# A gated delta rule with an SMELU MLP on one core: list scheduling of all orders, 32-bit transposes and block inverses by substitution

## The chip, the cores and the metric

The kernel runs on one core of one Trainium2 chip. The metric is device time in microseconds (us) from launch to end; a run's own span, from its first to its last instruction, is about 1.7 us shorter. PE is TensorE (PEld its weight loads), DVE is VectorE, ACT is ScalarE, POOL is GpSimd, SP is SyncE, which only issues DMAs. ACT, PE and SP with a "q" behind the name are the sequencers issuing something. Lnnn is a line of the kernel that the profile belongs to. A "step" is 32 tokens of the recurrence; there are 24, and four batches of eight heads run side by side. An execution is called slow when it took over 1.5% longer than the fastest of the same kernel, and fast otherwise; ratios use fast executions alone.

## The reference

```python
def _attn_ref(q, k, v, beta, g):          # B, H, S, D = 4, 8, 768, 48
    k_n = k / (np.linalg.norm(k, axis=-1, keepdims=True) + 1e-06)
    state = np.zeros((B, H, D, D)); y = np.zeros_like(q)
    for t in range(S):
        readout = einsum('bhd,bhde->bhe', q[:, :, t], state)
        y[:, :, t] = g[:, :, t] * readout
        v_old = einsum('bhde,bhd->bhe', state, k_n[:, :, t])
        state = state + beta[:, :, t] * outer(k_n[:, :, t], v[:, :, t] - v_old)
    return y

def _moe_ref(x, w_in, w_out):             # 3072 tokens, 384 -> 2048 -> 384
    h = x @ w_in
    g = where(h >= 1, h, where(h <= -1, 0, (h + 1) ** 2 / 4))
    return g @ w_out
# out = _moe_ref(_attn_ref(...) as [B*S, H*D])
```

The recurrence is computed 32 tokens at a time. Each step needs the Gram matrix of its keys, the inverse of a 32x32 unit-triangular matrix for each of the 32 batch-head pairs, and four products with a 48x48 state. All of these are 32x32 matmuls: 32 to 64 of them for one logical product. The MLP is ordinary large matmuls on the readouts.

## The kernel before

A pair of steps is inverted by four Newton levels, each of two products with a copy through ACT or DVE behind each. The MLP has two PSUM buffers and starts when four steps are done. The framework's scheduler decides the order.

```python
    psS = ... bufs=1   # state
    psN = ctx.enter_context(tc.tile_pool(name="psN", bufs=2, space=bass.MemoryType.PSUM))   # Gram, Newton
    psC = ctx.enter_context(tc.tile_pool(name="psC", bufs=2, space=bass.MemoryType.PSUM))   # chain
    psM = ctx.enter_context(tc.tile_pool(name="psM", bufs=2, space=bass.MemoryType.PSUM))   # MLP
    # [...]
    def newton_pair(p):
        # [...]
        for lv in range(4):
            ep = psN.tile([128, 2, J, 32], FP, name=f"ep{p}_{lv}", tag="n")
            # [4 matmuls put 2*I into ep]
            for c in range(2):
                for j in range(J):
                    for h4 in range(4):
                        r = slice(32 * h4, 32 * h4 + 32)
                        nc.tensor.matmul(ep[r, c, j], zc[c][r, j], al[c][r, j], start=False, stop=True, ...)
            e16 = nwt.tile([128, 2, J, 32], F16, ...)
            nc.scalar.copy(out=e16[:], in_=ep[:])
            zp = psN.tile([128, 2, J, 32], FP, name=f"zp{p}_{lv}", tag="n")
            # [64 matmuls more, zp = e16^T zc, then a copy to z16 on DVE or ACT]
    # [...]
    def mlp_in(gi, xt, m):
        hp = psM.tile([128, NT], FP, name=f"hp{gi}_{m}", tag="m")      # NT = 512 tokens
        for kt_ in range(3):
            nc.tensor.matmul(hp[:], win[:, kt_, m * 128:m * 128 + 128], xt[:, kt_]..., ...)
        rl = ...; nc.scalar.activation(out=rl[:], in_=hp[:], func=AF.Relu, bias=c_half[:], scale=0.5)
        if m % 2 == 0:      # DVE: max, then min and product
            # [...]
        else:               # POOL squares, DVE finishes
            # [...]
    # [mlp_out: 16 matmuls of 384 columns for each of 4 token tiles]
    # [...]
    for s in range(NSTEP):
        xt = chain_step(s)
        if s % 2 == 1:
            parallel(s // 2 + 2)          # loads, Gram, Newton of a later pair
        # [a share of the MLP tasks of the last complete group of four steps]
```

Of the kernel before, what the change touches and what calls it, by code (L numbers as in the profile page):

```python
# [9 lines left out]
U16 = mybir.dt.uint16  # L10
# [3 lines left out]


def _ap(t, dims, off=0):

    a = t[:]
    return bass.AP(tensor=a.tensor, offset=a.offset + off, ap=[list(a.ap[0])] + [list(d) for d in dims])


@with_exitstack
def kernel(
# [20 lines left out]
    NM = DFF // 128  # L44
    assert D == 48 and H == 8 and B == 4

    const = ctx.enter_context(tc.tile_pool(name="const", bufs=1))
    raw = ctx.enter_context(tc.tile_pool(name="raw", bufs=2))
    prep = ctx.enter_context(tc.tile_pool(name="prep", bufs=2))
    small = ctx.enter_context(tc.tile_pool(name="small", bufs=2))  # L50
    ktp = ctx.enter_context(tc.tile_pool(name="ktp", bufs=4))
    nwt = ctx.enter_context(tc.tile_pool(name="nwt", bufs=3))
    zfp = ctx.enter_context(tc.tile_pool(name="zfp", bufs=3))
    chn = ctx.enter_context(tc.tile_pool(name="chn", bufs=2))
    xtp = ctx.enter_context(tc.tile_pool(name="xtp", bufs=2))
    mlpt = ctx.enter_context(tc.tile_pool(name="mlpt", bufs=4))
    mlpg = ctx.enter_context(tc.tile_pool(name="mlpg", bufs=28))
    outp = ctx.enter_context(tc.tile_pool(name="outp", bufs=3))
    psS = ctx.enter_context(tc.tile_pool(name="psS", bufs=1, space=bass.MemoryType.PSUM))
    psN = ctx.enter_context(tc.tile_pool(name="psN", bufs=2, space=bass.MemoryType.PSUM))  # L60
    psC = ctx.enter_context(tc.tile_pool(name="psC", bufs=2, space=bass.MemoryType.PSUM))
    psM = ctx.enter_context(tc.tile_pool(name="psM", bufs=2, space=bass.MemoryType.PSUM))


    HS = 4 * S * D
    raws = {}

    def load(s0, n):

        ts = {}  # L70
        for nm, src in (("k", k), ("q", q), ("v", v), ("g", g)):
            t = raw.tile([128, GS, J, D], FP, name=f"r{nm}{s0}", tag=f"raw_{nm}")
            ts[nm] = t
        raws[s0] = ts

    def load_part(s0, off, n, names):
        ts = raws[s0]
        for nm, src in (("k", k), ("q", q), ("v", v), ("g", g)):
            if nm not in names:
                continue  # L80
            for h4 in range(4):
                for c in range(off, off + n):
                    a = bass.AP(tensor=src.tensor, offset=src.offset + h4 * S * D + (s0 + c) * C * D,
                                ap=[[D, C], [HS, J], [1, D]])
                    nc.sync.dma_start(out=ts[nm][32 * h4:32 * h4 + 32, c, :, :], in_=a)  # L85


    braw = const.tile([128, NG, C], FP, name="braw")
    for h4 in range(4):
        for j in range(J):  # L90
            a = bass.AP(tensor=beta.tensor, offset=beta.offset + h4 * S + j * 4 * S,
                        ap=[[C, GS], [GS * C, NG], [1, C]])
            nc.sync.dma_start(out=braw[32 * h4 + 4 * j:32 * h4 + 4 * j + 4, :, :], in_=a)  # L93
    load(0, GS)
    load_part(0, 0, 2, "k")
    load_part(0, 0, 2, "qv")

    ones = const.tile([128, 32], FP, name="ones")
    nc.gpsimd.memset(ones[:], 1.0)
    id32 = const.tile([128, 32], FP, name="id32")  # L100
    upf = const.tile([128, 32], F16, name="upf")
    lof = const.tile([128, 32], F16, name="lof")
    for h4 in range(4):
        r = slice(32 * h4, 32 * h4 + 32)
        nc.gpsimd.affine_select(out=id32[r, :], in_=ones[r, :], compare_op=ALU.is_equal, fill=0.0,
                                base=0, pattern=[[-1, 32]], channel_multiplier=1)
        nc.gpsimd.affine_select(out=upf[r, :], in_=ones[r, :], compare_op=ALU.is_gt, fill=0.0,
                                base=0, pattern=[[1, 32]], channel_multiplier=-1)
        nc.gpsimd.affine_select(out=lof[r, :], in_=ones[r, :], compare_op=ALU.is_gt, fill=0.0,
                                base=0, pattern=[[-1, 32]], channel_multiplier=1)  # L110
    i16 = const.tile([128, 32], F16, name="i16")
    nc.gpsimd.tensor_copy(out=i16[:], in_=id32[:])
    two_i = const.tile([128, 16, 32], F16, name="two_i")
    nc.gpsimd.tensor_scalar(out=two_i[:], in0=_ap(id32, [[0, 16], [1, 32]]), scalar1=2.0, scalar2=None, op0=ALU.mult)
    upmask = const.tile([128, J, 2, 32], F16, name="upmask")
    nc.gpsimd.tensor_copy(out=upmask[:].rearrange("p j a c -> p (j a) c"), in_=_ap(upf, [[0, 2 * J], [1, 32]]))
    lomask = const.tile([128, J, 32], F16, name="lomask")
    nc.gpsimd.tensor_copy(out=lomask[:], in_=_ap(lof, [[0, J], [1, 32]]))
    c_half = const.tile([128, 1], FP, name="c_half")
    nc.gpsimd.memset(c_half[:], 0.5)  # L120


    NZM, NA = 6, 4
    zms, als = [], []
    for i in range(NZM):
        t = const.tile([128, J, 2, 32], F16, name=f"zm{i}")
        nc.gpsimd.memset(t[:], 0.0)
        nc.gpsimd.tensor_scalar(out=t[:, :, 0, :], in0=_ap(id32, [[0, J], [1, 32]]), scalar1=-1.0, scalar2=None, op0=ALU.mult)
        zms.append(t)
    for i in range(NA):  # L130
        t = const.tile([128, J, 32], F16, name=f"al{i}")
        nc.gpsimd.tensor_copy(out=t[:], in_=_ap(id32, [[0, J], [1, 32]]))
        als.append(t)
    kqs = []
    for i in range(4):
        t = const.tile([128, 2, J, 4, 32], F16, name=f"kq{i}")
        nc.gpsimd.memset(t[:], 0.0)
        kqs.append(t)

    sb = const.tile([128, NG, J, GS], FP, name="sb")  # L140
    bt = const.tile([128, NG, C], FP, name="bt")
    nc.vector.transpose(out=bt[:].rearrange("p a b -> p (a b)"), in_=braw[:].rearrange("p a b -> p (a b)"))  # L142
    nc.scalar.activation(out=sb[:].rearrange("p a b c -> p (a b c)"), in_=bt[:].rearrange("p a b -> p (a b)"), func=AF.Sqrt)

    load_part(0, 2, 2, "kqv")
    load_part(0, 0, 4, "g")


    win = const.tile([128, 3, DFF], F16, name="win")
    wout = const.tile([128, NM, DM], F16, name="wout")  # L150

    def load_weights():
        for h4 in range(4):
            for p0, kt, h2, e0, n in ((0, 0, 0, 0, 32), (0, 1, 0, 32, 16), (16, 1, 1, 0, 16), (0, 2, 1, 16, 32)):
                r0 = (h2 * 4 + h4) * D + e0
                nc.gpsimd.dma_start(out=win[32 * h4 + p0:32 * h4 + p0 + n, kt, :], in_=moe_w_in[r0:r0 + n, :])  # L156
        nc.gpsimd.dma_start(out=wout[:], in_=moe_w_out.rearrange("(m p) n -> p m n", p=128))


    st = {}  # L160

    def prep_pair(p):
        s0 = 2 * p
        gi, off = s0 // GS, s0 % GS
        rw = raws[gi * GS]
        kr = rw["k"][:, off:off + 2]
        sbv = _ap(sb, [[1, 2], [GS, J]], gi * J * GS + off)
        ksq = prep.tile([128, 2, J, D], FP, name=f"ksq{p}", tag="ksq")
        nc.gpsimd.tensor_tensor(out=ksq[:], in0=kr, in1=kr, op=ALU.mult)  # L169
        nsq = small.tile([128, 2, J], FP, name=f"nsq{p}", tag="nsq")  # L170
        nc.vector.tensor_reduce(out=nsq[:], in_=ksq[:], axis=AX.X, op=ALU.add)  # L171
        nrm = small.tile([128, 2, J], FP, name=f"nrm{p}", tag="nrm")
        nc.scalar.activation(out=nrm[:], in_=nsq[:], func=AF.Sqrt)
        nre = small.tile([128, 2, J], FP, name=f"nre{p}", tag="nre")
        nc.vector.tensor_scalar(out=nre[:], in0=nrm[:], scalar1=1e-6, scalar2=None, op0=ALU.add)
        rcp = small.tile([128, 2, J], FP, name=f"rcp{p}", tag="rcp")
        nc.vector.reciprocal(out=rcp[:], in_=nre[:])
        rs = small.tile([128, 2, J], FP, name=f"rs{p}", tag="rs")
        nc.vector.tensor_tensor(out=rs[:], in0=rcp[:], in1=sbv, op=ALU.mult)  # L179
        kq = kqs[p % 4]  # L180
        kqf = kq[:].rearrange("p s j a t -> p (s j) (a t)")
# [4 lines left out]
        for c in range(2):  # L186
            nc.gpsimd.tensor_tensor(out=vt[:, c], in0=rw["v"][:, off + c],
                                    in1=_ap(sb, [[GS, J], [0, D]], gi * J * GS + off + c), op=ALU.mult)
        st[p] = dict(kq=kq, vt=vt, kt=[], zm=[], al=[])

    def gram_step(p, c):
        d = st[p]
# [208 lines left out]
```

## Time and profile before

Median 608.07 us (five runs, 603.64 to 611.33), profiled span 600.9 us, mean granted clock 0.730.

| | before |
|---|---|
| PE matmuls, busy | 14,496, 364.9 us (61%) |
| DVE, ACT, POOL busy | 37%, 25%, 25% |
| first matmul, last matmul, end of span | 34.3, 597.6, 600.9 us |
| sum over blocks of 256 PE instructions of max(3.6 us, own run time) | 499 us (own run time alone: about 350) |
| rest between first and last matmul | 64 us |

The sum in the fourth row is called the block sum below. A block's own run time in it is an estimate: 0.0080 or 0.0125 us for each small matmul with its weight load, at full or half clock, and 0.216 us for 512 columns of a large one at full clock (rates from these traces). The "rest" is the time from the first matmul's start to the last one's end, less the block sum, and the "tail" is what follows the last matmul. A recount with the same rates came within about 2% of every block sum given here; the 350 hangs more on how the matmuls that put 2*I into ep, four side by side, are counted (a recount gives 319 to 389).

From the page: the matmul row, the queue table and the shares of the chain of waits. In the queue table the columns are packets, MB, and share of 16 DMA engines' span.

```profile
PE 364.9 (61%) x14496; PEld 213.9 (36%) x14496; DVE 222.2 (37%) x360; ACT 149.5 (25%) x253; POOL 147.7 (25%) x168
...
q8 instruction: 113, 1.85, 1.3%
...
issue 42%; PE 24%; SPq 9%; POOL 8%; DVE 7%; ACT 5%; DMA 4%; POOLq 0%; ACTq 0%
```

No engine is full, and the chain leads with "issue": time in which an engine waited for nothing that the profile shows. The 14,496 matmuls and as many weight loads are 28,992 PE instructions; 28,992 / 256 = 113.25, and there are 113 packets of 1.85 MB / 113 = 16 KB.

The timeline of PE inside a stretch of small matmuls (start, us, what; in brackets, idle time before it and what ended it):

```profile
175.15 0.32 PE L226 MATMUL ep_2_3853<-al_213,z_1_3851 32*32 32x32 f16 x21 [1.15 <-issue]
175.31 0.43 PE L226 MATMUL ep_2_3853<-al_215,z_1_3851 32*32 32x32 f16 x32
175.56 0.49 PE L292 MATMUL yp_4297<-s_3320,kt_2196 32*32 32x48 f16 x30
176.51 0.53 PE L234 MATMUL zp_2_3924<-z_1_3851,e_2_3922 32*32 32x32 f16 x45 [0.46 <-ACT e_2_3922 L228]
178.88 0.32 PE L234 MATMUL zp_2_3924<-z_1_3851,e_2_3922 32*32 32x32 f16 x19 [1.84 <-issue]
...
182.33 0.23 PE L297 MATMUL yp_4297<-u_4229,zm_203 32*32 32x48 f16 x5 [1.47 <-issue]
...
186.06 0.23 PE L263 MATMUL kp_4449<-s_4295,kt_2265 16*32 16x48 f16 x5 [2.36 <-issue]
```

Count from one "issue" to the next: 21 + 32 + 30 + 45 = 128 matmuls, that is 256 instructions with their weight loads. Even a single product (L234) is cut in the middle, 45 matmuls before the stop and 19 after. The restarts lie 3.73, 3.45 and 3.73 us apart, though the work between them needs about 1.6 us (estimate: 128 times 0.0125). The reading from this is that a block of 256 PE instructions costs about 3.6 us or its own run time, whichever is longer.

The other loss, in the MLP's last group (same columns):

```profile
572.00 0.81 PE L316 MATMUL hp_7_16626<-xt_15576,win 128*128 128x512 f16 x3 [1.97 <-DVE gt_5_16612 L328]
572.65 0.81 PE L316 MATMUL hp_8_16636<-xt_15576,win 128*128 128x512 f16 x3
575.49 0.81 PE L316 MATMUL hp_9_16646<-xt_15576,win 128*128 128x512 f16 x3 [2.03 <-DVE gt_7_16632 L328]
```

Two tiles run, then PE waits 2 us for the DVE operation that frees a PSUM buffer two tiles back: 3.49 us for two tiles that need 1.3.

### The profile page before, as it was taken

Reading aid. Unit: us, or ns where it says so; the run is one execution under the profiler, and the core shown is the slowest. Engines: PE = TensorE matmul, PEld = TensorE weight load, DVE = VectorE, ACT = ScalarE, POOL = GpSimd, SP = SyncE. Lnnn points to the kernel's source line nnn. Section 1 sums busy time; section 2 is a strip of 40 time slices with the busy share of each in tenths; the row PEclk is TensorE's granted clock in tenths of the full one; section 3 lists DMA queues with packets and bytes.
Section 4 is the critical chain, followed back from the end, with each engine's and each line's share of the span. In section 5 each row is a group of like instructions: output and inputs, shape, how many; then the busy total and the mean of one; then the engine's idle time right before and its main releaser. Section 6 shows DMA issues by size and latency. Waiting matters only on the chain.

```text
span 600.9 us, 30600 instructions
## 1 busy us (share of the span) xinstructions
PE 364.9 (61%) x14496; PEld 213.9 (36%) x14496; DVE 222.2 (37%) x360; ACT 149.5 (25%) x253; POOL 147.7 (25%) x168
## 2 busy tenths in 40 slices
PE   0033544658745647646877566877476875678637
PEld 0022433214433413433443443444333533444314
DVE  0131312655102435313744224744037542254351
ACT  1001111421221222222313133313234122243331
POOL 9962000635000122100611102502014321022220
PEclk9999999967855555556585557885558965578899
DMA  1797433550100000024430024410034400000101
GB/s 21 133 177 123 72 73 70 99 98 17 34 5 4 3 0 5 3 47 77 76 76 3 5 60 87 78 55 4 4 75 84 108 4 4 17 5 15 39 1 52
DMA packets 111629, 28.81 MB, mean 48 GB/s; under 512 B 106000, under 2 KB 111120, under 8 KB 111504
## 3 DMA queue, kind: packets, MB, share of 16 engines
q1 hardware_dynamic: 108800, 23.72, 20.1%
q0 software_dynamic: 2704, 3.15, 3.3%
q8 instruction: 113, 1.85, 1.3%
q14 instruction: 12, 0.10, 0.1%
HBM read 25.26 MB, written 4.72 MB: 50 GB/s over the span
## 4 chain that ended last, share of the span: by engine, by line
issue 42%; PE 24%; SPq 9%; POOL 8%; DVE 7%; ACT 5%; DMA 4%; POOLq 0%; ACTq 0%
SPq L85 8%; DMA rg_139<-in_g_dram 2%; SPq L93 2%; PE sps L280 1%; DMA rk_136<-in_k_dram 1%; DMA rv_138<-in_v_dram 1%; PE op_3_6904 L334 1%; PE op_0_9639 L334 1%; PE op_0_12434 L334 1%; PE op_1_6864 L334 1%; PE op_2_6884 L334 1%; PE op_3_16776 L334 0%; PE op_2_16756 L334 0%; PE op_3_16536 L334 0%; PE op_2_16516 L334 0%
## 5 line engine op out<-in xcount | busy, mean ns | idle before, releaser
L316 PEld LDWEIGHTS <-win 128*128 128x128 f16 x288 | 31.6, 117 | 105.7 <-issue 95.8
L203 PE MATMUL gp_291<-kt_289 32*32 32x64 f16 (+1 forms) x64 | 1.0, 236 | 34.3 <-DVE kt_289 L195 34.3
L182 POOL TENSOR_TENSOR kq_217<-rk_4716,rs_4794 128x768 f16<-128x768 f32 x1 | 1.5, 1475 | 56.6 <-DVE rs_4794 L179 56.6
L203 PEld LDWEIGHTS <-kt_289 32*32 32x32 f16 (+1 forms) x64 | 0.9, 122 | 34.3 <-DVE kt_289 L195 34.3
L327 POOL TENSOR_TENSOR r_1_4415<-rl_1_4412 128x512 f32<-128x512 f32 x1 | 1.1, 1050 | 47.1 <-ACT rl_1_4412 L319 47.1
L221 PEld LDWEIGHTS <-i_181 32*32 32x32 f16 x192 | 5.8, 96 | 10.1 <-DVE al_209 L209 5.2
L327 POOL TENSOR_TENSOR r_11_8621<-rl_11_8618 128x512 f32<-128x512 f32 x1 | 1.0, 1038 | 33.6 <-ACT rl_11_8618 L319 33.6
L280 PEld LDWEIGHTS <-kq_221 32*32 32x32 f16 x384 | 5.8, 107 | 7.4 <-issue 7.4
L156 POOL DMA_DIRECT2D win<-in_moe_w_in_dram x16 | 8.2, 516 | 0.0
L327 POOL TENSOR_TENSOR r_5_15903<-rl_5_15900 128x512 f32<-128x512 f32 x1 | 1.0, 1039 | 27.3 <-ACT rl_5_15900 L319 27.3
L280 PEld LDWEIGHTS <-kq_217 32*32 32x32 f16 x384 | 5.9, 110 | 5.0 <-issue 5.0
L327 POOL TENSOR_TENSOR r_5_13883<-rl_5_13880 128x512 f32<-128x512 f32 x1 | 1.0, 1038 | 26.1 <-ACT rl_5_13880 L319 26.1
L327 POOL TENSOR_TENSOR r_7_11108<-rl_7_11105 128x512 f32<-128x512 f32 x1 | 1.0, 1038 | 25.8 <-ACT rl_7_11105 L319 25.8
L171 DVE TENSOR_REDUCE nsq_274<-ksq_272 128x16 f32<-128x768 f32 x1 | 1.0, 954 | 13.6 <-POOL ksq_272 L169 13.6
L182 POOL TENSOR_TENSOR kq_219<-rk_136,rs_1006 128x768 f16<-128x768 f32 x1 | 1.5, 1474 | 16.4 <-DVE rs_1006 L179 16.4
L280 PEld LDWEIGHTS <-kq_219 32*32 32x32 f16 x384 | 4.5, 104 | 2.9 <-issue 2.9
L142 DVE STREAM_TRANSPOSE bt<-braw 128x192 f32<-128x192 f32 x1 | 0.4, 379 | 13.2 <-DMA braw<-in_beta_dram 13.2
L238 DVE CAST z_2_839<-zp_2_774 128x512 f16<-128x512 f32 x1 | 0.7, 692 | 12.3 <-PE zp_2_774 L234 12.3
L327 POOL TENSOR_TENSOR r_1_15595<-rl_1_15592 128x512 f32<-128x512 f32 x1 | 1.0, 1039 | 16.8 <-ACT rl_1_15592 L319 16.8
L327 POOL TENSOR_TENSOR r_1_12800<-rl_1_12797 128x512 f32<-128x512 f32 x1 | 1.0, 1039 | 16.1 <-ACT rl_1_12797 L319 16.1
L280 PEld LDWEIGHTS <-kq_223 32*32 32x32 f16 x320 | 3.7, 101 | 2.9 <-issue 2.9
L238 DVE CAST z_2_1563<-zp_2_1498 128x512 f16<-128x512 f32 x1 | 0.7, 690 | 10.6 <-PE zp_2_1498 L234 10.6
(1828 smaller groups left out, 1186.1 us busy)
## 6 DMA issues: line engine op xcount, KB each, us to landing
wout<-in_moe_w_out_dram POOLq DMA_DIRECT2D x1, 1536.0 KB, 16.4
win<-in_moe_w_in_dram POOLq DMA_DIRECT2D x8, 128.0 KB, 4.5
rk_136<-in_k_dram SPq DMA_DIRECT2D x16, 48.0 KB
rq_137<-in_q_dram SPq DMA_DIRECT2D x16, 48.0 KB
rv_138<-in_v_dram SPq DMA_DIRECT2D x16, 48.0 KB
rg_139<-in_g_dram SPq DMA_DIRECT2D x16, 48.0 KB
rk_2111<-in_k_dram SPq DMA_DIRECT2D x16, 48.0 KB
rq_2112<-in_q_dram SPq DMA_DIRECT2D x16, 48.0 KB
```

The lines of the kernel that those rows point to most:

```text
L85: nc.sync.dma_start(out=ts[nm][32 * h4:32 * h4 + 32, c, :, :], in_=a)
L93: nc.sync.dma_start(out=braw[32 * h4 + 4 * j:32 * h4 + 4 * j + 4, :, :], in_=a)
L156: nc.gpsimd.dma_start(out=win[32 * h4 + p0:32 * h4 + p0 + n, kt, :], in_=moe_w_in[r0:r0 + n, :])
L171: nc.vector.tensor_reduce(out=nsq[:], in_=ksq[:], axis=AX.X, op=ALU.add)
L182: nc.gpsimd.tensor_tensor(out=kqf[:, :, 0:D], in0=kr.rearrange("p s j d -> p (s j) d"), in1=_ap(rs, [[1, 2 * J], [0, D]]), op=ALU.mult)
L203: nc.tensor.matmul(gp[r, j], kt[rk, j, ch, :], kt[rk, j, ch::2, :], start=(ch == 0 and j == 0), stop=(ch == 1), skip_group_check=True)
L221: nc.tensor.matmul(ep[r], i16[r, :], two_i[r], start=True, stop=False, skip_group_check=True)
L238: nc.vector.tensor_copy(out=z16[:], in_=zp[:])
L280: nc.tensor.matmul(sps[r, ch, j * D:j * D + D], kq[r, j, ch, :], u16[r, j], start=(s == 0 and j == 0), stop=True, skip_group_check=True)
L316: nc.tensor.matmul(hp[:], win[:, kt_, m * 128:m * 128 + 128], xt[:, kt_].rearrange("p b t -> p (b t)"), start=(kt_ == 0), stop=(kt_ == 2))
L327: nc.gpsimd.tensor_tensor(out=r2[:], in0=rl[:], in1=rl[:], op=ALU.mult)
L334: nc.tensor.matmul(op[:], gts[gi, m][:, b * GS * C:(b + 1) * GS * C], wout[:, m, :], start=(m == 0), stop=(m == NM - 1))
```

## The change

The intent is to take work off PE and to have every engine's order fixed by a planner inside the kernel. The inverse of a 32x32 block becomes two 16x16 inverses by substitution on POOL (DVE for the first group) and one merge on PE; the readout of a step runs as filler behind the next step's chain; transposes move two 16-bit values as one 32-bit word; the MLP works on units of two or four steps, with six PSUM banks shared by all. The diff, cut to its core:

```diff
-        for lv in range(4):                       # newton_pair: 528 matmuls for two steps
-            [ep: 68 matmuls, copy on ACT, zp: 64 matmuls, copy on DVE or ACT]
+        for jj in range(1, 15):                   # inverse of four steps: substitution, no PE
+            P.add(sub, d, ..., tensor_tensor(out=tm, in0=x column, in1=x row, op=ALU.mult))
+            P.add(sub, d, ..., tensor_tensor(out=x rows, in0=x rows, in1=tm, op=ALU.add))
+        P.add("PE", pe_dur(128), D2 + 0.1, mm1, [av, d0v], [pp], "fill", ...)     # the merge:
+        P.add("ACT", ..., p16 <- pp)                                              # 2 x 128 matmuls
+        P.add("PE", pe_dur(128), D2 + 0.4, mm2, [pvv, zv], [of], "fill", ...)     # for four steps
-        nc.vector.transpose(out=kt[:]..., in_=d["kq"][:, c]...)
+        nc.vector.transpose(out=kt[:].bitcast(FP)..., in_=kqt[:, c].bitcast(FP)...)
-    psN, psC, psM with two PSUM buffers each
+    bank = [psp.tile([128, 512], FP, name=f"bank{i}") for i in range(6)]   # chosen by the planner
-                nc.sync.dma_start(out=ts[nm][...], in_=a)
+        if eng == "SP" and kind == "load":
+            alt = [("ACT", dur, lambda ...: nc.scalar.dma_start(out=tile_, in_=src))]
-        [scheduler of the framework; MLP by groups of four steps]
+    UNITS = [2, 2, 4, 4, 4, 4, 2, 2]              # steps in each MLP unit
+    order = P.run(NB, pol)                        # list scheduling by a table of durations
+    with tc.manual_schedule():
+        for t in order: t.fn()
-        nc.sync.dma_start(out=out[r0:r0 + GS * C, :], in_=ot[:])
+            # a unit of two steps: 64 rows of each of two batches in one store
+                dst = bass.AP(..., ap=[[S * DM, 2], [DM, 64], [1, DM]])
+            P.add("SP", 0.46, -60, lambda ...: nc.sync.dma_start(out=dst, in_=ot[:]), [ov], [], "store", ...)
[...]
```

The planner's table charges 7.6 ns for a small matmul and knows nothing of stops at block ends. PE matmuls fall to 9,792; the MLP's columns on PE stay the same.

## The prediction

> **What bounds the kernel before.** No engine is full: the page gives PE 61%, DVE 37%, ACT and POOL 25% of 600.9 us. The chain of waits puts 42% on "issue". The timeline of PE shows what that is: wherever small 32x32 matmuls run, PE stops 1.2 to 2.4 us after every 128 matmul/weight-load pairs (restarts at 171.4, 175.2, 178.9, 182.3 us), with no semaphore to wait for. The DMA table has a queue of kind "instruction": 113 packets, 1.85 MB, so 16 KB or 256 instructions each. I read the stops as PE waiting for its instructions. The Trainium skill, "Runtime: NRT & Kernel Launch", section "Instruction fetch mechanics", gives the same 16 KiB blocks but calls the crossing "mostly hidden"; this trace disagrees: a block of 128 small pairs needs 1.6 us at half clock and takes 3.6. Charging each block max(3.6 us, its own run time) gives 499 us of the 564 from the first matmul (34.3) to the last; about 45 of the rest are MLP waits on two PSUM buffers (PE waiting for DVE), as in 205-225 and 560-586.
>
> Clock: the page's early 1.00 is wrong, since 512-column matmuls at 104 us start 0.42 us apart (half clock). Later records change in steps of 3.41 us: up after a window that streams over about 75%, down below about 36%.
>
> **What the change does.**
> - The Newton inverse (6336 small matmuls, serial PE-ACT-PE-DVE) becomes substitution on POOL (DVE for the first group) plus 1536 small matmuls. PE matmuls fall from 14,496 to 9,792, blocks from 113 to about 77: the main gain.
> - MLP columns on PE are unchanged (123 us at full clock, from 0.216 us per 512 columns), but start after two steps instead of four, with six PSUM banks, interleaved with the chain.
> - 32-bit transposes: 0.7 instead of 1.2 us (estimate); MLP elementwise on DVE: one 0.69 us operation per tile instead of 1.5. DVE, ACT and POOL then need 6 to 9 us per step each: off the critical path.
>
> **Estimate.** I took the new PE order in blocks of 256 instructions, charged 0.0080/0.0125 us per small pair (full/half clock, from 64-matmul groups of the trace), columns at the clock for the large ones, and at least 3.6 us per block. All at full clock: 322 us; at half: 430; with the clock rule above: 336. Such a sum for the old order gives 482 against 564; without its 45 us of buffer waits, about 7% was missing. So 336 + 20. First matmul about 21 us instead of 34; the first inverse and load issues on ACT ahead of it cost about 12 more; tail 3.5; the timed value lies 7 above the span: about 395 us.
>
> **What would show it.** "Instruction" packets about 76; PE still stopping about 2 us "issue" per 128 small pairs, and "issue" still leading the chain of waits; no step faster than about 11 us; first MLP matmul at 55-65 instead of 104 us; the 12-20 us MLP stretches with two-buffer waits gone; mean clock 0.75 to 0.9; PE about 60% busy.
>
> **What would make it wrong.** If the fetch can run several blocks ahead while large matmuls give it time, the time falls towards 300. If the fixed order, planned without fetch stops, makes engines wait for each other, or loads issued from ACT hold up the chain, or the clock stays at half: 440 and more.
>
> Chances: faster by over 2% 0.98, within 2% 0.01, slower 0.01. Predicted 395 us, 350 to 440.

## The result, and the profile after

The time after is 419.30 us (median of five, 417.61 to 426.50) against 608.07: ratio 0.6886, 95% interval 0.6846 to 0.6926. A ratio is the mean time of one kernel's fast runs over that of the other's fast runs of the same rounds, so it isn't quite the ratio of the medians. The profiled run of the changed kernel, 426.5 us, is slow; its four other runs are fast (417.6 to 419.4). In the experiments below, the kernel that differs only in how stores are issued (e10) keeps the order of all else, and its trace is fast; where a reading of this trace matters, it was checked against that one.

| | before | after | difference |
|---|---|---|---|
| PE matmuls | 14,496 | 9,792 | |
| first matmul | 34.3 us | 21.5 us | -12.8 |
| sum of max(3.6 us, own run time) over blocks | 499 us | 342 us (e10: 340) | -157 |
| rest between first and last matmul | 64 us | 49 us (e10: 45) | -15 |
| last matmul to end | 3.3 us | 11.9 us | +8.6 |
| span | 600.9 us | 424.8 us | -176 |
| mean granted clock | 0.730 | 0.823 | |

The same lines of the page after:

```profile
PE 261.1 (61%) x9792; PEld 167.7 (39%) x9792; DVE 170.4 (40%) x318; ACT 167.5 (39%) x301; POOL 140.3 (33%) x261
...
q8 instruction: 76, 1.25, 1.2%
...
PE 54%; DMA 19%; issue 17%; DVE 3%; POOL 2%; ACT 2%; SPq 1%; ACTq 1%
```

There are 37 packets fewer, and 37 x 3.6 = 133 us is most of the 157 that the block sum lost. This is an account, not an experiment: no run puts the old inverse back into the new kernel, and e9 shows that a smaller block sum can turn into other waits. PE has the same share of a span that is 29% shorter. In stretches without MLP, its timeline has the same stops as before:

```profile
168.14 0.50 PE L654 MATMUL bank<-s,kt 24*32 24x48 f16 x29
170.97 0.54 PE L654 MATMUL bank<-s,kt 24*32 24x48 f16 x35 [2.33 <-issue]
171.30 0.52 PE L660 MATMUL bank<-u,ms 32*32 32x48 f16 x32
171.62 0.69 PE L562 MATMUL bank<-d,ab 16*32 16x16 f16 x61
174.97 0.68 PE L562 MATMUL bank<-d,ab 16*32 16x16 f16 x67 [2.65 <-issue]
```

Again 35 + 32 + 61 = 128 matmuls from stop to stop, and 4.0 us from restart to restart. The list of PE's waits after (what, released by what: us in total, times, longest):

```profile
PE bank L562 <- DVE d L552: 25.7, 1, 25.7
PE bank L494 <- DVE nn L467: 21.5, 1, 21.5
PE bank L494 <- issue: 10.7, 5, 2.8
...
PE bank L575 <- ACT p L373: 8.0, 1, 8.0
...
PE bank L699 <- issue: 4.7, 3, 2.2
```

L699 is the first MLP product. Its largest group of waits is now 4.7 us of "issue": the waits for DVE behind a PSUM buffer, 2 us for every two tiles before, are gone. In their place stand two waits at the start, 25.7 and 8.0 us, for the first inverse and its merge. Why they are so long is in ACT's timeline, which also shows the loads that ACT issues (ACTq):

```profile
21.63 5.01 ACTq L390 DMA_DIRECT2D rg<-in_g_dram  x4
26.68 0.38 ACT L373 ACTIVATE ab<-bank 128x256 f16<-128x256 f32 x1 [5.55 <-DMA rg<-in_g_dram]
...
36.49 0.38 ACT L373 ACTIVATE ab<-bank 128x256 f16<-128x256 f32 x1 [9.42 <-DMA rg<-in_g_dram]
...
42.53 0.66 ACT L373 ACTIVATE ab<-bank 128x256 f16<-128x256 f32 x2 [5.65 <-DMA rk<-in_k_dram]
...
58.07 5.72 ACTq L390 DMA_DIRECT2D rv<-in_v_dram  x8
63.97 0.84 ACT L373 ACTIVATE ksq<-rk 128x768 f32<-128x768 f32 x1 [20.79 <-DMA rv<-in_v_dram]
...
64.72 0.58 ACT L373 ACTIVATE p<-bank 128x512 f16<-128x512 f32 x1
```

The "ab" copies move the first Gram matrices out of PSUM; their matmuls ran at 21.5 to 30 us. The copies come at 26.7, 36.5 and 42.5 us, because loads stand ahead of them in ACT's order and wait for buffers and DMAs. The copy "p" of the merge comes at 64.7, behind loads for later groups. The first product of the chain (L627) starts at 67.4 us. The end of the chain of waits (start, us, what):

```profile
403.15 4.56 PE bank L725 x28
...
407.74 0.50 ACT ot L373
...
408.26 7.79 DMA out_dram<-ot
```

The last results wait for stores: 7.8 us for one DMA, and the last matmul ends 11.9 us before the span does. The tail is 11.9 us in the fast traces of e2, e3 and e4 too.

### The profile page after: what moved, and what is told of

Same layout as the page of the kernel before. It is cut to its first block, busy times and chain, and to the rows that moved or that the text cites. A ratio compares the mean times of both kernels' runs of the same rounds, so it can differ in the third digit from the quotient of the medians.

```text
span 424.8 us, 21311 instructions
## 1 busy us (share of the span) xinstructions
PE 261.1 (61%) x9792; PEld 167.7 (39%) x9792; DVE 170.4 (40%) x318; ACT 167.5 (39%) x301; POOL 140.3 (33%) x261
## 4 chain that ended last, share of the span: by engine, by line
PE 54%; DMA 19%; issue 17%; DVE 3%; POOL 2%; ACT 2%; SPq 1%; ACTq 1%
PE bank L699 18%; PE bank L725 16%; DMA rk<-in_k_dram 5%; DMA rg<-in_g_dram 5%; PE sps L638 4%; DMA rq<-in_q_dram 4%; DMA rv<-in_v_dram 3%; PE bank L654 3%; PE bank L494 3%; PE bank L611 3%; PE bank L627 2%; DMA out_dram<-ot 2%; PE bank L575 2%; PE bank L660 2%; PE bank L562 1%
## 5 line engine op out<-in xcount | busy, mean ns | idle before, releaser
L699 PE MATMUL bank<-xt,win 128*128 128x512 f16 (+1 forms) x384 | 94.1, 381 | 5.9 <-issue 4.7
L725 PE MATMUL bank<-wout,gt 128*128 128x384 f16 x384 | 87.5, 366 | 0.6 <-DVE gt L708 0.6
L708 DVE SCALAR_TENSOR_TENSOR gt<-bank,r 128x512 f16<-128x512 f32 x96 | 63.4, 681 | 47.1 <-ACT r L373 32.6
L373 ACT ACTIVATE rl<-bank 128x512 f32<-128x512 f32 x96 | 56.4, 596 | 58.3 <-PE bank L699 55.7
L705 POOL TENSOR_TENSOR r<-rl 128x512 f32<-128x512 f32 x25 | 26.0, 1041 | 116.6 <-ACT rl L373 96.1
L725 PEld LDWEIGHTS <-gt 128*128 128x128 f16 x384 | 38.9, 107 | 34.1 <-issue 14.9
L699 PEld LDWEIGHTS <-win 128*128 128x128 f16 x384 | 39.2, 109 | 32.0 <-issue 15.6
L494 PE MATMUL bank<-kt 24*32 24x64 f16 x1536 | 22.3, 217 | 37.5 <-DVE nn L467 21.5
L373 ACT ACTIVATE r<-rl 128x512 f32<-128x512 f32 x71 | 43.9, 629 | 1.6
L494 PEld LDWEIGHTS <-kt 24*32 24x32 f16 x1536 | 19.0, 109 | 41.0 <-DVE nn L467 21.5
L562 PE MATMUL bank<-d,ab 16*32 16x16 f16 x768 | 7.8, 173 | 34.8 <-DVE d L552 25.7
L638 PE MATMUL sps<-u,kq 32*32 32x48 f16 x1472 | 18.6, 194 | 16.5 <-ACT u L373 8.6
L373 ACT ACTIVATE u<-bank 128x384 f16<-128x384 f32 x24 | 11.8, 490 | 42.5 <-PE bank L627 34.6
L535 POOL TENSOR_TENSOR xx<-xx,tm 128x28 f32<-128x28 f32 (+6 forms) x70 | 24.3, 347 | 5.2
L638 PEld LDWEIGHTS <-kq 32*32 32x32 f16 x1472 | 15.4, 98 | 25.5 <-issue 24.8
L532 POOL TENSOR_TENSOR tm<-xx 128x28 f32<-128x28 f32 (+6 forms) x70 | 23.5, 335 | 4.9
```

The source lines that it names most:

```text
L373: nc.scalar.activation(out=out, in_=in_, func=func, **kw)
L494: nc.tensor.matmul(b[32 * h4:32 * h4 + 32, 64 * j:64 * j + 64], _apr(kt, 32 * h4, 24, [[2, 32]], j * 128 + par), _apr(kt, 32 * h4, 24, [[2 ...
L532: P.add(sub, d, D0 + 0.1 * jj, lambda jj=jj, n=n, tm=tm: seng.tensor_tensor(out=_ap(tm, [[n * jj, 2], [jj, n], [1, jj]]), in0=_ap(x, [[256 ...
L535: P.add(sub, d, D0 + 0.1 * jj, lambda jj=jj, n=n, tm=tm: seng.tensor_tensor(out=_ap(x, [[256, 2], [16, n], [1, jj]], (jj + 1) * 16), in0=_ ...
L638: nc.tensor.matmul(sps[32 * h4:32 * h4 + 32, par, D * j:D * j + D], _apr(kqt, 32 * h4, 32, [[2, 32]], (c * J + j) * 128 + par), u16[32 * h ...
L699: nc.tensor.matmul(b[:, x * nt:x * nt + nt], win[:, kt_, m * 128:m * 128 + 128], xt[:, kt_ * nt:kt_ * nt + nt], start=(kt_ == 0), stop=(kt ...
```

## The experiments

Twelve kernels ran; all gave correct results. Times are medians; each comparison names the runs of the same rounds where it can, since the kernel before itself takes 600.5 to 609.0 us from chip to chip.

### e1: the changed kernel again

No edit; the reference for e2 to e4.

> The changed kernel again, unedited, for a trace in the fast state and as the base of the other runs of this call. Both theories: 417 to 421 us fast, 76 instruction packets, first chain product (the up matmuls) near 67 us; the tail after the last matmul shorter than the 12 us of the slow trace, 4 to 8 us.

421.82 us, ratio 0.6971 (0.6924 to 0.7019). Its profile again fell in the slow state (span 424.9 us), so it can't show whether the tail is shorter in the fast one, as was expected; e2 to e4 show that it isn't. The block sum is 343, the rest 49, so the account above repeats.

### e2: no loads from ACT

```diff
-        if eng == "SP" and kind == "load":
+        if False:
             alt = [("ACT", dur, ...)]
```

> No load is issued from ACT; SP issues all. Theory A (ACT works in order, and its load issues, slowed while the DMA engines are full, stand in front of the copies ab and p16 that the first inverse needs): the chain starts at 44 to 52 us instead of 67, time 15 to 22 us less, about 400 us. Rival B (the DMA traffic itself sets the start, whoever issues it): the chain still starts after 62 us, time within 5 us of the unedited kernel.

400.60 us, ratio 0.6643 (0.6593 to 0.6694), that is 21 us less than e1. The start in its PE timeline:

```profile
43.08 1.19 PE L562 MATMUL bank<-d,ab 16*32 16x16 f16 x128 [14.90 <-DVE d L552]
...
48.73 0.50 PE L627 MATMUL bank<-rr,zz 32*32 32x48 f16 x32 [0.84 <-DVE zz L580]
```

The first product of the chain starts at 48.7 instead of 67.4 us, 18.7 us earlier. The inverse itself still makes PE wait 14.9 us, instead of 25.7. In ACT's timeline the copies now wait for PE alone: the last "ab" comes at 28.2 instead of 42.5 us, and "p" right behind the product that it copies.

```profile
28.23 0.38 ACT L373 ACTIVATE ab<-bank 128x256 f16<-128x256 f32 x1 [0.47 <-PE bank L494]
...
44.36 0.60 ACT L373 ACTIVATE p<-bank 128x512 f16<-128x512 f32 x1 [15.75 <-PE bank L562]
```

That 18.7 is close to the 21 us gained doesn't show that the start is the whole gain. The edit isn't pure, since the planner also reorders later work: by the fifth step the lead over e1 is down to 4.5 us (its product with u, L638, starts at 126.9 against 131.4), with SP's load issues at 37% of the chain of waits from 70 to 128 us, and it grows again later. Between the two profiled spans (28 us, e1's slow), the first matmul gives 5, the blocks of the start 14 and a smaller block sum 13 (330 against 343); 4 to 5 are lost to other waits.

### e3: 64 tiny matmuls more in each step

```diff
             b = bk(gp)
+            for j in range(16):
+                for h4 in range(4):
+                    nc.tensor.matmul(b[32*h4:32*h4+32, 0:1], <24 rows of kt, 32 columns>,
+                                     <one column of kt>, start=True, stop=True, ...)
             for par in range(2):
```

Before each Gram product, 64 matmuls of one column; the Gram product then overwrites their result. They add 24 x 128 = 3,072 instructions, 12 blocks, and next to no columns.

> 64 extra 24x32 matmuls of one column per step ahead of each gram, into its own bank, overwritten at once: 1536 pairs, 3072 instructions, 12 more instruction blocks; the result stays right. Theory fetch (3.6 us per 256 instructions): plus 35 to 45 us, 88 instruction packets. Rival execution (PE time per pair, 8 to 12.5 ns): plus 12 to 19 us.

455.11 us, ratio 0.7535: 33 us more than e1. The queue table has twelve packets more:

```profile
q8 instruction: 88, 1.44, 1.3%
```

PE's busy time rose by 18 us. The block sum rose by 43 (343 to 386), the 12 x 3.6 that was expected; the rest fell from 49 to 33, so part of it went into waits that were there anyway. The time went slightly under the expected 35 to 45, and far above what the tiny matmuls' run time explains.

### e4: three large matmuls more in each step

```diff
             b = bk(gp)
+            for j in range(3):
+                nc.tensor.matmul(b[:, 0:384], <128 columns of kt>, <384 columns of kt>,
+                                 start=True, stop=True, ...)
```

In the same place, 27,648 columns, 11.7 us of PE at full clock (0.216 us for 512), in 144 instructions, about half a block.

> 3 extra 128x128 matmuls of 384 columns per step in the same place, 0.49 us at full clock and 0.98 at half, as much PE time as the 64 tiny ones or more, but only 144 instructions in all. Theory fetch: plus 0 to 8 us, since blocks of small matmuls have 1 to 2 us of idle time while the next block is fetched. Rival execution: plus 12 to 24 us, at least as much as the tiny ones.

421.28 us, ratio 0.6950 (0.6892 to 0.7007): no difference from e1, though these intervals would hide some 4 us. PE's busy time rose from 260.9 to 274.7 us; the packets rose by one:

```profile
q8 instruction: 77, 1.26, 1.2%
```

So 11.7 to 23 us of PE's work (estimate, by the clock) cost nothing, while 12 blocks of almost no work cost 33 us. What PE pays for in these stretches is the number of instructions. (Every matmul here has a weight load of its own, so matmuls and instructions can't be counted apart.) That it is the fetch which holds it is an inference from the packets of 16 KB, the count of 256 and the absence of any semaphore; no record shows PE waiting for a packet by name.

### e5: stores of 64 rows, with e2

```diff
-                dst = bass.AP(..., ap=[[S * DM, 2], [DM, 64], [1, DM]])
-            t = P.add("SP", 0.46, -60, <one store>, ...)
+                parts = [(0, 64, 2*x*S + s0*C), (64, 64, (2*x+1)*S + s0*C)]
+            for p0, np_, r0 in parts:
+                dst = bass.AP(..., ap=[[DM, np_], [1, DM]])
+                t = P.add("SP", 0.46, -60, <a store of ot[p0:p0+np_]>, ...)
```

> On top of e2: the store of an output tile of a two-step unit is split into two stores of 64 rows each, instead of one of 2 x 64 rows. Theory (the outer dimension of 2 keeps such a store on 2 of the 16 DMA engines, and the last four queue up behind each other): the tail from the last matmul to the end falls from 12 us to 4 to 5 us, time 6 to 9 us below e2, about 392 us. Rival (the stores are slow for another reason, such as the number of rows of 1.5 KB or the two output buffers): within 3 us of e2.

397.55 us, ratio 0.6640 against e2's 0.6643: no gain that can be measured, where 6 to 9 us was expected. The tail did fall from 11.9 to 4.2 us, but each store became two tasks, the planner chose another order, and the block sum rose from 330 to 339. The experiment changed two things; e10 takes the order out of it.

### e10: the same stores, order unchanged

The task stays one, and issues two stores of 64 rows when it runs; nothing else differs from the changed kernel.

> The changed kernel with each 2 x 64 row store issued as two stores of 64 rows, the order of everything else unchanged (so without the reordering that spoiled e5). Theory (2 of 16 DMA engines per such store): 7 to 9 us less than the changed kernel, 411 us or so; the wait of the last output copies for the stores gone, tail 4 us instead of 12. Rival: no gain.

410.51 us, ratio 0.6827 (0.6776 to 0.6878), between 0.9% below the changed kernel's own rounds (0.6886) and 2.1% below e1's (0.6971). These are other chips, so the clean number is inside the traces: last matmul to end is 4.2 us (406.4 to 410.6) instead of 11.9. The last two copies before a store, on ACT, after and then in e10:

```profile
412.23 0.49 ACT L373 ACTIVATE ot<-bank 128x384 f32<-128x384 f32 x1 [4.00 <-DMA out_dram<-ot]
416.14 0.49 ACT L373 ACTIVATE ot<-bank 128x384 f32<-128x384 f32 x1 [3.43 <-DMA out_dram<-ot]
```

```profile
403.86 0.49 ACT L373 ACTIVATE ot<-bank 128x384 f32<-128x384 f32 x1 [2.16 <-PE bank L725]
406.46 0.49 ACT L373 ACTIVATE ot<-bank 128x384 f32<-128x384 f32 x1 [2.11 <-PE bank L725]
```

After, each waits for an earlier store to give its buffer back; in e10 they wait only for PE. DMA is busy to 5 to 12% in the tail of the changed kernel (one or two of 16 engines), and to 20 to 31% in e10. The Trainium skill, "DMA: Bandwidth & Descriptors", section "Why a DMA increments its semaphore by 16 and not by 1", says that a DMA uses the largest number of engines, up to 16, that divides the slowest dimension of both sides; here that dimension is 2 on one side. The share of the changed kernel's tail agrees with it.

### e6: the planner charges the stops

e5, and the time that the planner reckons for PE counts instructions and holds each 256 at 3.6 us at least:

```diff
+    def fetched(self, t, s, d):
+        [...]
+            if self.pc % 256 == 0:
+                now = max(now, self.entered + 3.6); self.entered = now
```

> On top of e5: the planner charges 3.6 us for each 256 PE instructions when it orders the work; policy the same. Theory fetch floor (each block costs the larger of 3.6 us and its own run time, and the sum over the order is 332 us against 336 for e5): within 5 us of e5. Rival (the fixed order was made for the wrong times, so engines wait for each other): 10 to 25 us below e5.

423.81 us, ratio 0.7042: 26 us slower than e5, where both theories expected otherwise. The block sum is unchanged (338 against 339), the rest rose from 36 to 64. The shares of its chain of waits:

```profile
PE 39%; SPq 25%; issue 13%; DMA 11%; POOL 5%; DVE 3%; ACT 2%; ACTq 0%; DVEq 0%; POOLq 0%
```

And the longest group of PE's waits:

```profile
PE bank L524 <- DVE kt L514: 45.9, 7, 16.2
```

SP issues the 384 loads at 0.55 to 0.6 us each, about 220 us in all, and with ACT's help gone (e2) this queue leads the stalls of the chain. The Gram products wait for the transposed keys (kt), those for the loads. But e5 has the same queue, and no slower: SP had issued 144 loads by 100 us in e5 and 148 in e6, 294 and 298 by 200 us. In e5 the waits for kt were 24.0 us in two pieces, and those of L638 for ACT's u 4.9 us, where e6 has 23.1 (L668 there). So the new order meets the loads and ACT worse; why it does is not shown, and the cause of the 26 us stays open.

### e7 and e8: MLP spread among the small matmuls

If a block costs max(3.6 us, own run time), then large matmuls are cheapest inside blocks that would stop anyway. e7 is e6 with a credit: each small instruction earns a share of the remaining MLP work, and an MLP tile runs when it is earned. e8 is e7 with units of two steps throughout, so that the MLP starts early and never runs out; it also lets filler work run one step earlier.

```diff
+        if ml is not None and self.credit >= 0.3 and rm <= free + 0.15:
+            return ml, max(rm, free)
[...]
+            self.credit = min(1.5, self.credit + rate * t.ni)
-UNITS = [2, 2, 4, 4, 4, 4, 2, 2]
+UNITS = [2, 2, 2, 2, 2, 2, 2, 2, 2, 2, 2, 2]       # e8 only, with TAIL = 14
```

> On top of e6: PE takes MLP matmuls evenly between the small ones (a credit per small instruction) instead of a quota per step. Same instructions, same run time. Theory fetch floor: large matmuls fill the time in which PE waits for the next block of instructions, the sum of max(3.6 us, run time) falls from 332 to 305 us, so 20 to 30 us below e6; clock up from 0.82 to 0.87 or more; same 76 instruction packets. Rival (PE time or the latency of the chain binds): no gain, or slower, since the chain is delayed by MLP work.

> As e7, with MLP units of two steps throughout and a shorter planned tail: 300 us by the same sum, so 3 to 8 us below e7; more weight loads for the same columns (77 packets). If the elementwise engines or the number of output stores bind, no gain.

e7 took 399.82 us (0.6680), 24 less than e6: the block sum fell from 338 to 305, the rest was 72. e8 took 394.03 us (0.6523; two of four runs slow): block sum 304, rest 63. In both, SP's queue leads the stalls with 29% of the chain. So mixing took the 33 us off the block sum that the block rule says, but the time gained only on e6: against e5, in the same rounds, e7 gains nothing (399.82 to 397.55 us), and e8 1.8% with intervals that overlap. What the block sum lost went to the rest (36 us in e5, 72 in e7).

### e11: e8 with some loads on ACT again

Loads go to ACT too, except those of the stretch in which the first inverse waits for ACT (by the planner's urgency D, between -36.5 and -2.5):

```diff
-        if False:
+        if eng == "SP" and kind == "load" and (D < -36.5 or D > -2.5):
             alt = [("ACT", dur, ...)]
```

The run changed one thing more than its text says: the planner charges a load's issue 0.57 us instead of 0.46.

> e8 with loads allowed on ACT again, except those of the first groups other than the first 16 (so none stands before the first inverse). Theory (in e7 and e8 the loads, all issued from SP at about 0.55 us each until 215 us, pace the first half): 10 to 25 us below e8, about 375 us; the share of SP issue in the chain of waits falls from 29% to under 12%. Rival (the chain is paced by the inverse on POOL, or ACT is delayed by its loads again): within 5 us of e8 or slower.

370.53 us, ratio 0.6141 (0.6084 to 0.6198): the fastest of all, 23 us under e8 of other rounds and, by the ratios, 11% under the changed kernel. The block sum stayed (303), the rest fell from 63 to 41; SP's queue fell to 11% of the chain. That the loads paced e8 is thus well supported, though the two edits weren't tried apart. A piece of its PE timeline:

```profile
171.83 0.25 PE L667 MATMUL sps<-u,kq 32*32 32x48 f16 x11 [1.68 <-issue]
172.01 0.83 PE L728 MATMUL bank<-xt,win 128*128 128x256 f16 x6
172.68 0.81 PE L754 MATMUL bank<-wout,gt 128*128 128x384 f16 x4
173.42 0.67 PE L640 MATMUL bank<-s,kt 24*32 24x48 f16 x64
174.02 0.83 PE L728 MATMUL bank<-xt,win 128*128 128x256 f16 x6
...
179.01 0.25 PE L683 MATMUL bank<-s,kt 24*32 24x48 f16 x11 [0.57 <-issue]
```

From one "issue" to the next, 256 matmuls pass, two blocks, in 7.2 us. That is still 3.6 us for each, but MLP tiles now fill the time; the stretch shown of the kernel before has four stops in 11 us.

### e9: the kernel before with two Newton levels

```diff
-        for lv in range(4):
+        for lv in range(2):
```

One part of the change alone: fewer small matmuls, and nothing else. (With two levels the result is still within the tolerance on these inputs.)

> The kernel before with 2 Newton levels instead of 4, nothing else: 3168 matmuls and as many weight loads fewer, 24.8 of 113 instruction blocks; the result may be slightly or clearly wrong on purpose. Theory fetch (3.6 us per block of small matmuls): 75 to 95 us less than before, 88 or 89 instruction packets. Rival execution (12.5 ns per pair at half clock): 40 us less. It does not tell the fetch from the serial latency of the two levels, about 3 us each per pair of steps, which would give up to 75 us if none of it were covered.

576.32 us, ratio 0.9589: 24 us less than before, where the block rule promised 75 to 95 and the rival, PE's run time, 40; neither was met. The packets fell from 113 to 88 and the block sum from 499 to 416, the full 83 us. But the rest rose from 64 to 121. The list of PE's waits:

```profile
PE hp L316 <- DVE gt L328: 74.9, 36, 3.2
...
PE hp L316 <- DVE mx L323: 28.2, 22, 1.6
```

MLP tiles wait 103 us for their two PSUM buffers; before, this was 58. The gain turned into another wait.

### e12: the same, with a third PSUM buffer for the MLP

```diff
-    psN = ctx.enter_context(tc.tile_pool(name="psN", bufs=2, ...))
+    psN = ctx.enter_context(tc.tile_pool(name="psN", bufs=1, ...))
-    psM = ctx.enter_context(tc.tile_pool(name="psM", bufs=2, ...))
+    psM = ctx.enter_context(tc.tile_pool(name="psM", bufs=3, ...))
```

> The kernel before with two Newton levels, as in e9, and one thing more: the PSUM bank that the Newton and Gram products had as their second goes to the MLP tiles, which then have three instead of two. Theory: what e9 failed to give (excess over the sum of max(3.6 us, own run time) rose from 64 to 120 us) is PE waiting for one of the MLP's two PSUM buffers; with three, these waits (103 us of PE before hp tiles in e9) fall by a third to a half, the excess by 20 to 40 us, and the time to 535 to 560 us. Rival: PE would have been held there anyway by the speed of DVE and ACT or by the fetch, and the bank taken from the Newton products makes those wait for one another: no change from e9 (576 within 2%), or slower.

572.08 us against 608.97 of its rounds, ratio 0.9367: 2.3% under e9 by the ratios, about 14 us. The expected 535 to 560 was missed. The waits did fall as expected, from 103 to 60 us:

```profile
PE hp L316 <- DVE gt L328: 52.1, 40, 3.0
...
PE hp L316 <- DVE mx L323: 8.0, 9, 1.6
```

The rest fell with them, from 121 to 91. But the block sum rose from 416 to 444: with more buffers the scheduler ran the MLP in fewer, denser pieces, and 78 blocks instead of 71 were left that hold too little work for 3.6 us. So the buffers did hold the MLP, and about half of what they gave back (by the ratios; nearly all by the two profiled spans, 573.9 and 572.5 us on different chips) was lost to unmixed blocks. The rival, that nothing would move, holds for the time within its 2% almost as well; it fails for the waits.

## Why the prediction was right or wrong

The time, 419.3 us, lies in the range of 350 to 440, 24 us above the predicted 395.

**Right: what bounds the kernel.** The stops per 256 instructions and the queue of 16 KB packets were read from the profile before; e3 and e4 confirm that instructions, and not PE's work, are what costs. The packet count was predicted as about 76 and is 76. The block sum was predicted as 336 us and is 342. By this account the term is 157 of the 176 us by which the span shrank.

**Right: the MLP waits go away, the clock rises.** L699 has no group of DVE waits over 1 us. The mean clock is 0.82 (0.75 to 0.9 predicted), PE is busy 61%. How much of the 15 us in the rest is due to the six banks and how much to the interleaving wasn't separated; e9 and e12 show only that fewer instructions alone, or with one buffer more, bring 4 to 6%.

**Mis-sized: the start.** The step in the prediction is "the first inverse and load issues on ACT ahead of it cost about 12 more". The first matmul came at 21.5 us as predicted (21). But the three blocks that hold the first Gram products, the inverse and the merge exceed the block rule by 3.4 + 24.0 + 5.6 = 33 us, so this term was 21 too small. e2 shows a good part of the cause: without loads on ACT the same three blocks exceed the rule by 18 us, so ACT's loads made about 15 of the 33. The 18 that are left, 14.9 of them PE waiting for the inverse while SP alone loads, are by themselves more than the 12 predicted for both. I had named the mechanism and sized it as if ACT's load issues only took their own time; they also wait, in order, for the buffers and DMAs that they need, and the copies behind them wait too. The first MLP matmul, too, came at 83 us, not at 55 to 65; in e2 it comes at 63. What the start is worth in the end isn't shown, since e2's lead shrank and grew again.

**Mis-sized: the tail.** The step is "tail 3.5". It took 11.9 us, 8.4 more, and e10 brings it to 4.2. The diff shows the store's new outer dimension of 2, and the skill's page (named under e10) states what follows from it; I didn't look the store up, as it was off the critical path everywhere but at the end.

**Smaller terms.** "The timed value lies 7 above the span" compared a median with another run's span; within one run it is 1.7, so this term was 5.3 too large. The terms as written add up to 399.5, not 395, which the text didn't say. Against the profiled (slow) run, the account closes: 399.5 + 0.5 (first matmul) + 6.3 (block sum) + 17.1 (everything over the block rule: 49.1 against 20 + 12) + 8.4 (tail) - 5.3 = 426.5. The 17.1 is the start's +21 and about -4 elsewhere.

**Wrong: what leads the chain.** "'issue' still leading the chain of waits" failed: it is 17%, behind PE (54%) and DMA (19%). The stops are still there, as the timeline shows, but the chain now runs through MLP matmuls for much of the span, and through the start's loads. The stops' share of a chain isn't the number to predict them by; the block count is.

**Wrong: "no step faster than about 11 us".** Of the 22 intervals between the state products (L638) of successive steps, 11 are shorter (10 in e10), the shortest 6.6 us. A step has 376 small matmuls on average, 2.9 blocks, but they aren't bound to it: between two state products PE ran from 256 to 1,012 matmuls, since Gram, inverse and readout move between the steps.

**What would have made it wrong.** The prediction listed loads on ACT that hold up the chain; this happened at the start. It didn't foresee that the same loads also relieve SP: in e2 the lead of the start is mostly lost again while SP issues all loads, and e11 gains by giving ACT a part of them.

## What to carry to other kernels

Where a timeline shows PE stopping without a semaphore after a fixed count of instructions, cost the kernel in blocks of that count, each at the longer of the stop's period and its own run time; then remove instructions, and put large matmuls among small ones rather than beside them: this took the block sum from 339 to about 304 us (e7 and e8 against e5), though the time followed only when the loads were shared too (e11). After cutting one term, look for what the freed time runs into: new waits, above all those for two PSUM buffers, took 57 of 83 us in e9, and the load queue of a single issuing engine held e8 until e11 shared it. A load on a computing engine's queue costs not its issue time but everything that it waits for, so keep it away from the one stretch where a short copy of that engine is on the chain (about 15 us at the start here).

## What the Trainium skill lacked or had wrong

- "Runtime: NRT & Kernel Launch", section "Instruction fetch mechanics", calls the crossing of a 16 KiB boundary "mostly hidden". Its blocks of 256 instructions agree with the traces (113 packets before, 76 after). The cost doesn't: for small matmuls a block took about 3.6 us where its work needs 1.6, and 12 blocks more cost 33 us (e3). No page gives a rate for the fetch.
- "TensorE: Matmul & The Clock Gate", Part 1, says that start-to-start "never drops below ≈25 ns however small N is". With 32x32 matmuls on four row groups, 64 of them start within 0.54 us before (182.47 to 183.01 us), about 8.4 ns each or 34 ns for four. So the sentence can hold at most for one tile position. It doesn't say so there; the same page's Part 3 does let matmuls at different tile positions start about 4 ns apart, and the two passages aren't tied together.
- The same Part 1 gives windows of 3.4 us and a clock of half or full; the records agree (steps of 3.41 us, 0.5 or 1.0). It doesn't say how busy a window must be. Counted over the windows of the traces before and after (columns at the granted clock, the four row groups of small matmuls side by side), 26 of 27 rises came after a window that streamed 76% of it or more, one at 70%; all 29 falls came after 38% or less, and no window that kept the full clock was below 38%. The upper limit isn't sharp: about a dozen windows between 75 and 84% stayed at half clock.
- "DMA: Bandwidth & Descriptors", section "Issuing engines are not separate DMA queues", says that issuing from several engines only saves the sequencer's time, "usually small relative to the DMA itself". One issue is: a load of 48 KB in 256 pieces took 0.55 to 0.6 us to issue and 2.3 to 2.6 us to land (e6). But 384 issues from SP alone add up, to 25 to 29% of the chain in e6 to e8 (11% and 23 us less in e11). "Perfetto Trace Analysis", "DMA Optimizations", does advise balancing in such a case; it doesn't warn that a load on ACT holds up the computing behind it (about 15 us at the start, e2).
- The rule for the number of DMA engines ("DMA: Bandwidth & Descriptors") was right and was missed: the outer dimension of 2 made a tail of 11.9 us, and 4.2 without it.
